# Second products summed in PSUM, and the transposes of x cut into pieces, in a fused attention and feed-forward kernel

## The chip, the cores and the metric

The kernel runs on one core of one Trainium2 chip. The metric is the device time of one execution in microseconds. Three runs of the kernel before took 543.70, 538.14 and 542.87 us, median 542.87. TensorE does the matrix products, VectorE (DVE), ScalarE (ACT) and GpSimd (POOL) do the elementwise work, and SyncE (SP), ACT and POOL issue the DMAs.

## The reference

There are 8 batches of 448 tokens, 12 heads of width 64, and a model width of 768.

```python
scores = q @ k.transpose(0, 1, 3, 2) / sqrt(64)
attn   = maximum(scores, 0) ** 2 / 448
x      = (attn @ v), heads side by side           # 8 x 448 x 768
xn     = (x - mean(x)) / sqrt(var(x) + 1e-6) * g_ln
out    = x + maximum(xn @ w_ch1, 0) @ w_ch2       # 768 -> 3072 -> 768
```

All inputs and the output are fp32; the kernel computes its products in bf16.

## The kernel before, in words

Batches go in four pairs of 896 tokens. The order of all instructions is written by hand: each engine and each DMA queue runs its own in the order in which the program emits them, and waits for the others by semaphores.

Attention leaves x transposed, `xT`, with the model width on the partitions. The first layer reads it so. The output needs x with tokens on the partitions, 7 tiles of 128 tokens by 6 chunks of 128, so `tokens(pair)` (L635) transposes all 42 blocks of a pair with one DMA on SP's queue into `xtok`, a pool with one buffer. `statistics` (L643) makes mean and variance of a tile on DVE from it, `roots` the scale `rstd`; the scale is applied to the output of the second layer.

Pair 0's first layer is computed directly. Pairs 1 to 3 use `ffn1_pair` (L757): for each of 12 steps `n`, seven block products in place of eight, with sums of blocks of x (`start`, made by DVE, L789) and of blocks of the weights. Pair 1 makes the weight sums and stores them in DRAM (`kept`); pairs 2 and 3 fetch them again, the "early" ones on ACT's queue from step 3 on, the "late" ones on SP's (`fetch`, L783). In `run` (L915) three products are gathered in an SBUF tile `z` (L922 to L926), and DVE writes `z` minus a product back into that product's PSUM bank (L938, L941), onto which the last two products accumulate. After each step `between` may add work: `between_two` and `between_three` put the statistics of pairs 2 and 3 there, one tile to a step.

The second layer of pairs 0 and 1 is direct (`ffn2_units`) and lies beside the attention of pairs 1 and 2. That of pairs 2 and 3 uses seven products too: `ffn2_mid` does the middle token tile 3, then `ffn2_pair` (L1042) does the tile pairs (0, 4), (1, 5) and (2, 6). A product is 12 matmuls (L1061) and has two units, halves of six. In `ffn2_pair` the products come in the order 3, 2, 5, 4, 1, 6, 7, with sums held in five output buffers, eight for pair 3 (`next_out`); ACT copies three of them out of PSUM (L1128, L1133, L1137), DVE adds (L1130, L1141, L1146), POOL subtracts and adds (L1142, L1143), and the four results are scaled and added to x on ACT and POOL (L1121, L1122) and on DVE (L1118, L1152, L1155), then stored by SP. The last tile pair has an order of its own, `finish_early`. Sums of the ReLU output that the next tile pair needs (`following`, h_sums_of) are made by DVE as their places come free.

Pair 2's seven-product second layer lies beside the attention of pair 3. `interleave` spreads two lists over each other: the units of the second layer, and the bundles of attention, three score steps each (L365 scores, L376 ReLU on ACT, L380 or L378 square, L397 values, L403 eviction into `xT`). The hooks "even" and "odd" are emitted after the third and the fifth of six groups of heads. The last `few` = 5 units are held back until attention is done and `start` of the next first layer has made the sums of x. Then `tokens(pair + 1)` is issued, and `run` begins. Pair 3's second layer runs by itself at the end.

Of the kernel before, what the change touches and what calls it, by code (L numbers as in the profile page):

```python
# [9 lines left out]
ALU = mybir.AluOpType  # L10
# [18 lines left out]
def kernel(  # L29
# [22 lines left out]
    nc = tc.nc  # L52
    P = 128
# [30 lines left out]
    xtpool = ctx.enter_context(tc.tile_pool(name="xt", bufs=1))  # L84
# [84 lines left out]
    hold = xtpool.tile([P, K1, NT, P], bf16, tag="xtok", name="hold_sb")  # L169
    hold = hold.rearrange("p c t d -> p (c t d)")  # L170
# [463 lines left out]

    def tokens(pair):  # L635
        xtok[pair] = xtpool.tile([P, K1, NT, P], bf16, tag="xtok", name="xtok_sb")
        rstd[pair] = spool.tile([P, NT], fp32, tag="rstd", name="rstd_sb")
        moments[pair] = spool.tile([P, NT, nc.vector.BN_AGGR_DIM], fp32, tag="mv", name="mv")
        nc.sync.dma_start_transpose(
            xtok[pair].rearrange("p c t d -> p (c t) d"),  # L640
            xT[pair].rearrange("p c s -> p (c s)"))
# [365 lines left out]
    def ffn2_mid(pair, a, b):  # L1007
# [22 lines left out]
        for names in (("s2", "s5"), ("s1",), ("s6",), ("s7",)):  # L1030
            h_sums_of(pair, 0, names)
# [10 lines left out]
    def ffn2_pair(pair, t, two_banks, last):  # L1042
# [5 lines left out]
        fp = next_out  # L1048

        def banks():  # L1050
            return (ps[:, :DH] for ps in two_banks())
# [15 lines left out]
        def scaled_on(o, left, right, row, half=None):  # L1067
            u = t + 4 * row
            if half is not None:
                right = xtok[pair][:, :, u, half * HP:(half + 1) * HP]  # L1070
                o, left = (z.rearrange("p (c d) -> p c d", d=D) for z in (o, left))
            nc.vector.scalar_tensor_tensor(
                o, left, rstd[pair][:, u:u + 1], right, op0=ALU.mult, op1=ALU.add)

        def out_of(z, row, half):
            store(pair, t + 4 * row, slice(half * DH, (half + 1) * DH), z, (nc.sync, nc.scalar))

        def finish_early():


            a, b = banks()
            yield from product(3, a)
            d, e, c12, c21, q_ = (fp() for _ in range(5))
            o12, o21 = next_out(), next_out()
            nc.scalar.copy(d, a)
            yield from product(2, b)
            nc.vector.tensor_sub(d, d, b)
            yield from product(5, a, False)
            nc.scalar.copy(c12, a)
            nc.gpsimd.tensor_sub(e, d, c12)  # L1090
            scaled_on(o12, a, None, 0, 1)
            out_of(o12, 0, 1)
            yield from product(4, b, False)
            nc.scalar.copy(c21, b)
            nc.gpsimd.tensor_add(e, e, c21)
            scaled_on(o21, b, None, 1, 0)
            out_of(o21, 1, 0)
            a, b = banks()
            yield from product(1, a)
            nc.vector.tensor_add(q_, a, d)  # L1100
            scaled_on(q_, q_, None, 1, 1)
            scaled_on(e, e, None, 0, 0)
            yield from product(6, b)
            scaled_on(q_, b, q_, 1)
            out_of(q_, 1, 1)
            yield from product(7, a, False)
            scaled_on(e, a, e, 0)
            out_of(e, 0, 0)

        if last:  # L1110
            yield from finish_early()
            return

        def result(eng, z, row, half):
            u = t + 4 * row
            z3, x = z.rearrange("p (c d) -> p c d", d=D), xtok[pair][:, :, u, half * HP:(half + 1) * HP]
            if eng is nc.vector:
                eng.scalar_tensor_tensor(  # L1118
                    z3, z3, rstd[pair][:, u:u + 1], x, op0=ALU.mult, op1=ALU.add)
            else:  # L1120
                nc.scalar.mul(z, z, rstd[pair][:, u:u + 1])  # L1121
                eng.tensor_add(z3, z3, x)  # L1122
            store(pair, u, slice(half * DH, (half + 1) * DH), z, (nc.sync, nc.sync))

        a, b = banks()
        yield from product(3, a)
        d = fp()
        nc.scalar.copy(d, a)  # L1128
        yield from product(2, b)
        nc.vector.tensor_sub(d, d, b)  # L1130
        yield from product(5, a, False)
        c12 = fp()
        nc.scalar.copy(c12, a)  # L1133
        yield from product(4, b, False)
        following("s2")
        c21 = fp()
        nc.scalar.copy(c21, b)  # L1137
        a, b = banks()
        yield from product(1, a)
        q_ = fp()  # L1140
        nc.vector.tensor_add(q_, a, d)  # L1141
        nc.gpsimd.tensor_sub(d, d, c12)  # L1142
        nc.gpsimd.tensor_add(d, d, c21)  # L1143
        following("s1")
        yield from product(6, b)
        nc.vector.tensor_add(q_, q_, b)  # L1146
        result(nc.gpsimd, q_, 1, 1)
        following("s6")
        result(nc.vector, c12, 0, 1)
        result(nc.vector, c21, 1, 0)  # L1150
# [33 lines left out]
    def token_units(pair):  # L1184
        return ([lambda: tokens(pair)] + [lambda t=t: statistics(pair, t) for t in range(NT)]
                + [lambda: roots(pair, 0, NT)])
# [177 lines left out]
```

## Time and profile before

| | us |
|---|---|
| median of three runs | 542.87 |
| the profiled execution | 543.38 |
| its span, first to last instruction | 540.2 |
| TensorE matmuls busy | 512.4 (95%) |
| VectorE busy | 386.1 (71%) |
| ScalarE busy | 316.7 (59%) |
| GpSimd busy | 129.7 (24%) |

The profile is of one execution. Busy times of an engine are summed over the span; matmuls are pipelined, so a busy TensorE can still be waiting inside. A row of a group gives its line, engine, operation and tiles, then busy time, mean duration and the idle time before it with what ended it. The list of waits names who waited for whom. The chain that ended last follows the execution back from its last instruction. A row of stages gives the busy time of each engine in a stretch of the span, the TensorE clock that was granted there as a share of the full one, and the busy share of the DMA engines.

### The profile page before, as it was taken

What the parts mean: (1) busy time and instruction counts of PE and PEld (TensorE: products, weight loads), DVE (VectorE), ACT (ScalarE), POOL (GpSimd) and SP (SyncE); (2) the same over time, 40 slices, a digit from 0 to 9 for tenths busy, and PEclk for the clock granted to TensorE, in tenths of its full rate; (3) what the DMA queues carried; (4) which work ended last, traced back from release to release, by engine and by line L of the source; (5) the groups of instructions that cost most, each with busy time, mean ns of one, the idle gap of its engine ahead of it and who ended that gap; (6) DMA issues with size and microseconds to landing.
All of it is one profiled execution on the core that took longest, in us unless ns stands there. A gap on an engine that the chain in (4) does not pass through costs nothing.

```text
span 540.2 us, 11478 instructions
## 1 busy us (share of the span) xinstructions
PE 512.4 (95%) x4565; PEld 301.3 (56%) x4565; DVE 386.1 (71%) x718; ACT 316.7 (59%) x512; POOL 129.7 (24%) x167
## 2 busy tenths in 40 slices
PE   8999999999999999999999969999989895999996
PEld 6677779655555555555555435545444442555663
DVE  5775754598998888678876858866866755865773
ACT  6966774688683676565462547669778062671110
POOL 7434101111221565011012690002320200000331
PEclk9999999999999999999999999999999897999999
DMA  9999999999899766159749984119872395411123
GB/s 197 206 205 208 210 179 165 167 166 193 157 178 177 155 203 159 52 94 181 147 92 177 200 179 112 52 30 159 130 128 60 98 167 130 133 51 27 33 58 89
DMA packets 124390, 74.34 MB, mean 138 GB/s; under 512 B 79794, under 2 KB 120754, under 8 KB 124338
## 3 DMA queue, kind: packets, MB, share of 16 engines
q1 hardware_dynamic: 93906, 42.16, 39.1%
q0 software_dynamic: 26976, 25.50, 32.0%
q10 hardware_dynamic: 3456, 5.97, 4.5%
q8 instruction: 35, 0.57, 0.4%
q14 instruction: 17, 0.14, 0.1%
HBM read 63.70 MB, written 16.91 MB: 149 GB/s over the span
## 4 chain that ended last, share of the span: by engine, by line
PE 81%; DMA 6%; ACT 6%; DVE 4%; issue 2%; SPq 0%; ACTq 0%; DVEq 0%
PE m_ps L847 23%; PE o_ps L728 20%; PE m_ps L1061 8%; PE h_ps L669 7%; PE sc_ps L365 6%; PE av_ps L397 5%; ACT attn_sb L376 4%; PE o_ps L1061 3%; DMA xtok_sb<-xT_sb 3%; PE o_ps L1017 3%; PE h_ps L713 2%; DMA room<-kept 2%; PE h_ps L695 1%; ACT early L376 1%; DMA w_sum<-kept 1%
## 5 line engine op out<-in xcount | busy, mean ns | idle before, releaser
L376 ACT ACTIVATE attn_sb<-sc_ps 128x896 bf16<-128x896 f32 (+4 forms) x150 | 126.0, 901 | 45.0 <-PE sc_ps L365 39.4
L728 PE MATMUL o_ps<-w,hT_sb 128*128 128x384 bf16 x672 | 116.0, 326 | 0.0
L851 ACT ACTIVATE hT_sb<-m_ps 128x448 bf16<-128x448 f32 x144 | 78.3, 544 | 62.3 <-PE m_ps L847 59.6
L728 PEld LDWEIGHTS <-hT_sb 128*128 128x128 bf16 x672 | 63.0, 98 | 48.8 <-issue 10.1
L380 DVE TENSOR_TENSOR attn_sb<-attn_sb 128x896 bf16<-128x896 bf16 x98 | 61.3, 637 | 30.6 <-ACT attn_sb L376 30.0
L669 PE MATMUL h_ps<-x_room,w 128*128 128x256 bf16 (+2 forms) x384 | 43.8, 263 | 0.4 <-ACT early L376 0.3
L1061 PEld LDWEIGHTS <-hT_sb 128*128 128x128 bf16 x288 | 28.0, 98 | 23.3 <-issue 5.6
L847 PE MATMUL m_ps<-x_sum,w 128*128 128x448 bf16 x144 | 33.9, 357 | 7.0 <-DVE x_room L924 7.0
L938 DVE TENSOR_TENSOR m_ps<-x_room,m_ps 128x448 f32<-128x448 f32 x36 | 22.6, 629 | 22.8 <-ACT hT_sb L851 22.5
L847 PEld LDWEIGHTS <-w_sum 128*128 128x128 bf16 x240 | 23.4, 98 | 26.6 <-DMA w_sum<-kept 5.1
L669 PEld LDWEIGHTS <-w 128*128 128x128 bf16 x384 | 33.8, 97 | 7.3 <-issue 2.9
L403 DVE TENSOR_SCALAR xT_sb<-av_ps 128x896 bf16<-128x896 f32 (+2 forms) x30 | 27.0, 900 | 14.5 <-PE av_ps L397 14.4
L847 PEld LDWEIGHTS <-w 128*128 128x128 bf16 x216 | 21.1, 98 | 27.4 <-issue 7.8
L646 DVE BATCH_NORM_STATS2 stats<-xtok_sb 128x6 f32<-128x384 bf16 x56 | 28.4, 549 | 9.9 <-DMA xtok_sb<-xT_sb 9.9
L159 POOL DMA_DIRECT2D k_sb<-in_k_dram x15 | 10.7, 712 | 100.5 <-DMA kT_sb<-k_sb 79.8
L159 POOL DMA_DIRECT2D v_sb<-in_v_dram x20 | 14.3, 715 | 82.5 <-PE sc_ps L365 72.2
L922 ACT COPY x_room<-m_ps 128x448 f32<-128x448 f32 x36 | 19.1, 532 | 24.6 <-PE m_ps L847 24.0
L1061 PEld LDWEIGHTS <-x_room 128*128 128x128 bf16 x216 | 20.5, 98 | 18.0 <-issue 5.2
L365 PE MATMUL sc_ps<-qT_sb,kT_sb 64*64 64x448 bf16 x392 | 28.8, 358 | 1.1 <-ACT attn_sb L376 0.9
L397 PE MATMUL av_ps<-attn_sb,v_sb 64*64 64x448 bf16 (+2 forms) x532 | 27.2, 331 | 1.1 <-DVE attn_sb L380 0.6
L679 ACT ACTIVATE hT_sb<-h_ps 128x256 bf16<-128x256 f32 (+1 forms) x49 | 18.1, 368 | 16.0 <-PE h_ps L669 15.1
L378 ACT ACTIVATE attn_sb<-attn_sb 128x896 bf16<-128x896 bf16 x28 | 26.6, 950 | 0.9
(213 smaller groups left out, 868.4 us busy)
## 6 DMA issues: line engine op xcount, KB each, us to landing
out_dram<-o_room SPq DMA_DIRECT2D x82, 96.0 KB, 2.3
w<-in_moe_w_ch_dram POOLq DMA_DIRECT2D x12, 384.0 KB, 13.9
w<-in_moe_w_ch_dram POOLq DMA_DIRECT2D x4, 1152.0 KB, 20.2
q_sb<-in_q_dram POOLq DMA_DIRECT2D x20, 224.0 KB, 5.6
v_sb<-in_v_dram POOLq DMA_DIRECT2D x20, 224.0 KB, 5.6
k_sb<-in_k_dram POOLq DMA_DIRECT2D x15, 224.0 KB, 5.2
w_room<-kept SPq DMA_DIRECT2D x12, 192.0 KB, 3.2
kept<-room SPq DMA_DIRECT2D x4, 480.0 KB, 2.8
```

Source lines behind the costliest of these rows:

```text
L365: nc.tensor.matmul(ps[cols, r, o * w:(o + 1) * w], g["k"](i)[rows, cols], g["q"](i, r)[rows, blk[0]:sum(blk), cols], start=True, stop=True)
L376: nc.scalar.activation(a, ps[:, :, :len(slots) * w], ACTF.Relu)
L378: nc.scalar.activation(a, a, ACTF.Square)
L380: nc.vector.tensor_mul(a, a, a)
L397: nc.tensor.matmul(ps[cols, hh, :w], v_sb[rows, pr, j * D:(j + 1) * D], g["attn"][i][rows, r, :], start=(j == 0), stop=(j == J - 1))
L403: nc.vector.tensor_scalar_mul(x, ps[:, :, :w], score_scale)
L646: nc.vector.bn_stats(stats[:, n], xtok[pair][:, n * G:(n + 1) * G, t, :])
L669: nc.tensor.matmul(ps[:, :w + more], w1[:, c, ni * P:(ni + 1) * P], xc[b][:, c, s.start:s.stop + more], start=(c == 0), stop=(c == K1 - 1))
L728: nc.tensor.matmul(ps[:, :DH], hT[pair][:, ki, t * P:(t + 1) * P], w2[:, ki, cols], start=(o == 0), stop=(o == K2 - 1))
L847: nc.tensor.matmul(ps, *at, start=(first and c == 0), stop=(c == KQ - 1), skip_group_check=not first)
L851: nc.scalar.activation(hT[pair][:, n + KH * row, half * S:(half + 1) * S], ps, ACTF.Relu)
L1061: nc.tensor.matmul(ps, x[:, ki], y[ki] if isinstance(y, list) else y[:, ki], start=(first and ki == 0), stop=(ki == KH - 1), skip_group_ch ...
```

## The change

`ffn2_pair` takes the products in the order 1, 4, 3, 2, 5, 6, 7, for all tile pairs alike. Products 1, 4 and 3 are added up in one fp32 tile `z` in SBUF; product 2 accumulates onto 4 in its bank and product 5 onto 3, which gives two of the four results. DVE then writes `z` minus each of these banks back into it, and products 6 and 7 accumulate onto that, which gives the other two. Each result is one DVE operation from PSUM into an output buffer. The two tiles for `z` take the place of two output buffers, the five further ones of pair 3 are gone, and three remain.

The room of the transposed x is one fixed tile now. Pair 1's transpose stays whole. Those of pairs 2 and 3 go in pieces: for pair 2, tiles 0 to 2 at the hook "even" (six DMAs), tiles 3 to 6 two chunks at a time just before `run` and after its steps 0 and 1; for pair 3, tiles 0 and 1 at "odd", tiles 3 to 5 after steps 0 and 1, tile 2 after step 2 and tile 6 after step 3. The statistics of pair 3 start after step 3 and take the tiles in the order 0, 1, 3, 4, 5, 2, 6.

The middle tile makes the sum s1 first. Beside pair 3's attention one bundle is emitted before the first unit, and four units instead of five are held back.

```diff
-    xtpool = ctx.enter_context(tc.tile_pool(name="xt", bufs=1))
...
-    hold = xtpool.tile([P, K1, NT, P], bf16, tag="xtok", name="hold_sb")
-    hold = hold.rearrange("p c t d -> p (c t d)")
+    xt_room = wpool.tile([P, K1, NT, P], bf16, tag="xtok", name="xtok_sb")
+    hold = xt_room.rearrange("p c t d -> p (c t d)")
...
+    def tokens_part(pair, lo, hi, chunks):
+
+        for c in chunks:
+            nc.sync.dma_start_transpose(xt_room[:, c, lo:hi], xT[pair][:, c, lo * P:hi * P])
+
     def tokens(pair):
-        xtok[pair] = xtpool.tile([P, K1, NT, P], bf16, tag="xtok", name="xtok_sb")
+        tokens_room(pair)
+        nc.sync.dma_start_transpose(
+            xt_room.rearrange("p c t d -> p (c t) d"), xT[pair].rearrange("p c s -> p (c s)"))
+
+    def tokens_room(pair):
+        xtok[pair] = xt_room
         rstd[pair] = spool.tile([P, NT], fp32, tag="rstd", name="rstd_sb")
         moments[pair] = spool.tile([P, NT, nc.vector.BN_AGGR_DIM], fp32, tag="mv", name="mv")
-        nc.sync.dma_start_transpose(
-            xtok[pair].rearrange("p c t d -> p (c t) d"),
-            xT[pair].rearrange("p c s -> p (c s)"))
...
-        for names in (("s2", "s5"), ("s1",), ("s6",), ("s7",)):
-            h_sums_of(pair, 0, names)
+        for name in ("s1", "s2", "s6", "s7"):
+            h_sums_of(pair, 0, (name,))
...
-    def ffn2_pair(pair, t, two_banks, last):
+    def ffn2_pair(pair, t, two_banks, z, last):
...
-        fp = next_out
-
-        def banks():
-            return (ps[:, :DH] for ps in two_banks())
+        a, b = (ps[:, :DH] for ps in two_banks)
...
-        def scaled_on(o, left, right, row, half=None):
-            u = t + 4 * row
-            if half is not None:
-                right = xtok[pair][:, :, u, half * HP:(half + 1) * HP]
-                o, left = (z.rearrange("p (c d) -> p c d", d=D) for z in (o, left))
...
+        def result(ps, row, half):
+            u, o = t + 4 * row, next_out()
+            o3, ps3 = (x.rearrange("p (c d) -> p c d", d=D) for x in (o, ps))
             nc.vector.scalar_tensor_tensor(
-                o, left, rstd[pair][:, u:u + 1], right, op0=ALU.mult, op1=ALU.add)
-
-        def out_of(z, row, half):
-            store(pair, t + 4 * row, slice(half * DH, (half + 1) * DH), z, (nc.sync, nc.scalar))
-
-        def finish_early():
...
-        if last:
-            yield from finish_early()
-            return
-
-        def result(eng, z, row, half):
...
-        a, b = banks()
+                o3, ps3, rstd[pair][:, u:u + 1], xtok[pair][:, :, u, half * HP:(half + 1) * HP],
+                op0=ALU.mult, op1=ALU.add)
+            store(pair, u, slice(half * DH, (half + 1) * DH), o, (nc.sync, nc.scalar if last else nc.sync))
+
+        yield from product(1, a)
+        nc.scalar.copy(z, a)
+        following("s1")
+        yield from product(4, b)
+        nc.vector.tensor_add(z, z, b)
         yield from product(3, a)
-        d = fp()
-        nc.scalar.copy(d, a)
-        yield from product(2, b)
-        nc.vector.tensor_sub(d, d, b)
+        nc.vector.tensor_add(z, z, a)
+        yield from product(2, b, False)
+        result(b, 1, 0)
+        nc.vector.tensor_sub(b, z, b)
         yield from product(5, a, False)
-        c12 = fp()
-        nc.scalar.copy(c12, a)
-        yield from product(4, b, False)
+        result(a, 0, 1)
+        nc.vector.tensor_sub(a, z, a)
         following("s2")
-        c21 = fp()
-        nc.scalar.copy(c21, b)
-        a, b = banks()
-        yield from product(1, a)
-        q_ = fp()
-        nc.vector.tensor_add(q_, a, d)
-        nc.gpsimd.tensor_sub(d, d, c12)
-        nc.gpsimd.tensor_add(d, d, c21)
-        following("s1")
-        yield from product(6, b)
-        nc.vector.tensor_add(q_, q_, b)
-        result(nc.gpsimd, q_, 1, 1)
+        yield from product(6, b, False)
+        result(b, 1, 1)
         following("s6")
-        result(nc.vector, c12, 0, 1)
-        result(nc.vector, c21, 1, 0)
-        d3, x = d.rearrange("p (c d) -> p c d", d=D), xtok[pair][:, :, t, :HP]
-        nc.vector.scalar_tensor_tensor(
-            d3, d3, rstd[pair][:, t:t + 1], x, op0=ALU.mult, op1=ALU.add)
         yield from product(7, a, False)
-        nc.vector.scalar_tensor_tensor(
-            d, a, rstd[pair][:, t:t + 1], d, op0=ALU.mult, op1=ALU.add)
-        store(pair, t, slice(0, DH), d, (nc.sync, nc.sync))
+        result(a, 0, 0)
         following("s7")
...
-    def token_units(pair):
-        return ([lambda: tokens(pair)] + [lambda t=t: statistics(pair, t) for t in range(NT)]
-                + [lambda: roots(pair, 0, NT)])
+    def token_units(pair, order):
+        return [lambda t=t: statistics(pair, t) for t in order] + [lambda: roots(pair, 0, NT)]
...
-                        tokens=token_units(2)[1:])
+                        tokens=token_units(2, range(NT)))
...
+        if n < 2:
+            tokens_part(2, 3, NT, range(2 * n + 2, 2 * n + 4))
+        elif n > 2 and side["tokens"]:
+            side["tokens"].pop(0)()
+
+    def between_three(n):
+        if n == 0:
+            side.update(tokens=token_units(3, (0, 1, 3, 4, 5, 2, 6)))
+        if n < 4:
+            tokens_part(3, *((3, 6, range(3)), (3, 6, range(3, K1)), (2, 3, range(K1)), (6, 7, range(K1)))[n])
         if n > 2 and side["tokens"]:
             side["tokens"].pop(0)()
 
-    def between_three(n):
-        if n == 0:
-            side.update(tokens=token_units(3)[1:])
-        if n > 1 and side["tokens"]:
-            side["tokens"].pop(0)()
+    soon = {(1, "even"): (0, 3, range(K1)), (1, "run"): (3, NT, range(2)), (2, "odd"): (0, 2, range(K1))}
...
-                yield from ffn2_pair(pair, t, lambda: banks(t), pair == pairs - 1 and t == 2)
+                yield from ffn2_pair(pair, t, banks(t), zs[t % 2], pair == pairs - 1 and t == 2)
...
-            following[name]()
+                if pair:
+                    tokens_room(pair + 1)
+            if name != "run":
+                following[name]()
+            if (pair, name) in soon:
+                tokens_part(pair + 1, *soon[pair, name])
         if last:
             mm = [ps_mm.tile([P, 512], fp32, tag="mm", name="o_ps") for _ in range(2)]
-            outs += [x_room.rearrange("p b c s -> p (b c s)")[:, 3 * KH * P:3 * KH * P + 2 * DH].bitcast(fp32),
-                     room0[:, 9:].rearrange("p c n -> p (c n)").bitcast(fp32)]
+            zs = [x_room.rearrange("p b c s -> p (b c s)")[:, 3 * KH * P:3 * KH * P + 2 * DH].bitcast(fp32),
+                  room0[:, 9:].rearrange("p c n -> p (c n)").bitcast(fp32)]
...
-        few = 5 if last else 3
-        interleave(units[:-few], beside)
+        few = 4 if last else 3
+        interleave(units[:-few], beside, 0, 1 if last else 0)
...
         stage = following
-        tokens(pair + 1)
+        if pair == 0:
+            tokens(pair + 1)
+        hook("run")
         stage["run"]()
...
-    z = late[0].tile([P, 5, DH], fp32, tag="z", name="z_sb")
-    outs[3:] = [z[:, i] for i in range(5)]
```

39 lines of the change are left out of this document (1 added, 38 removed).

## The prediction

> **What bounds the kernel now.** I read the busy shares first, then cut the span by stages. The windows below are, in order: the seven-product first layer of pair 1, of pair 2 and of pair 3; the attention of pair 3 beside the second products of pair 2; two stretches right after a PE stall; the second products of pair 3 alone; and the attention of pair 2 beside the second layer of pair 1. Columns: window, length, busy us and count of PE, weight loads, DVE, ACT and POOL, granted clock, DMA share, GB/s.
>
> ```profile
> core 0: us, PE busy (x) PEld busy (x) DVE busy (x) ACT busy (x) POOL busy (x), PEclk, DMA share, GB/s
> 175.17:221.95 46.78, 46.78 (x249) 24.13 (x247) 38.69 (x74) 30.86 (x57) 23.63 (x32) 1.00 0.63 164
> 297.02:349.53 52.51, 47.36 (x248) 23.88 (x247) 39.72 (x76) 30.95 (x58) 23.29 (x25) 1.00 0.68 140
> 429.54:485.93 56.39, 49.41 (x248) 24.88 (x247) 37.55 (x71) 30.93 (x58) 0.54 (x1) 0.92 0.56 118
> 356.94:429.54 72.60, 65.24 (x598) 33.91 (x598) 52.04 (x71) 53.37 (x68) 14.61 (x16) 0.99 0.60 110
> 426.74:431.20 4.46, 4.46 (x17) 2.20 (x17) 3.79 (x5) 0.91 (x2) 3.18 (x3) 0.62 0.00 1
> 451.70:455.10 3.40, 3.40 (x10) 1.36 (x10) 2.76 (x5) 1.08 (x2) 0.00 (x0) 0.50 0.28 73
> 494.70:535.90 41.20, 41.12 (x254) 24.56 (x251) 25.45 (x34) 5.54 (x11) 10.32 (x8) 1.00 0.26 59
> 222.00:297.02 75.02, 75.02 (x679) 40.76 (x678) 56.49 (x104) 38.81 (x52) 9.30 (x13) 1.00 0.71 126
> ```
>
> TensorE sets the time: in most stages it is busy to the last tenth. The three first layers do the same matmuls, yet take 46.78, 52.51 and 56.39 us. So pair 2 loses 5.73 us and pair 3 9.61 us against pair 1; the first is all idle time, the second partly a low clock. The list of what PE waited for, and the chain of work that ended last (start, us, what), say on what.
>
> ```profile
> PE m_ps L847 <- DVE x_room L924: 7.0, 1, 7.0
> PE m_ps L847 <- DMA w_sum<-kept: 4.2, 2, 2.3
> PE o_ps L1061 <- DVE o_room L1141: 2.7, 1, 2.7
> PE o_ps L1061 <- ACT o_room L1133: 2.0, 2, 1.4
> ...
> PE sc_ps L365 <- ACT attn_sb L376: 0.9, 4, 0.3
> PE m_ps L847 <- DMA room<-kept: 0.9, 1, 0.9
> ...
> PE o_ps L1061 <- DVE room L739: 0.6, 1, 0.6
> ```
>
> ```profile
> 300.12 8.80 DMA room<-kept
> 308.96 3.88 PE m_ps L847 x20
> 312.85 6.14 DMA w_sum<-kept
> ...
> 414.17 0.69 PE sc_ps L365 x12
> 414.86 3.05 PE o_ps L1061 x18
> 418.47 1.14 PE o_ps L1061 x6
> 419.61 1.48 PE av_ps L397 x28
> 421.11 1.10 DVE xT_sb L403
> 422.52 0.55 issue
> 423.06 3.16 DVE x_sum L789 x4
> 426.74 3.01 PE o_ps L1061 x12
> ...
> 435.15 14.72 DMA xtok_sb<-xT_sb
> 449.89 1.03 DVE stats L646 x2
> 451.07 0.59 DVE x_room L924
> ```
>
> Three places, then. In pair 2 the weight sums come back from DRAM too late, 8.80 and 6.14 us each. In pair 3 DVE stands at the statistics of tile 0, whose transpose took 14.72 us, and L924, which PE needs, is queued behind them. At 422 to 427 DVE makes the five sums of x first, and L1141, which must leave a PSUM bank before the last product goes into it, comes after. The two transposes are the same instruction:
>
> ```profile
> L639 SPq DMA_TRANSPOSE xtok_sb<-xT_sb x4: 6557/9304/12465, 83.9 to 435.1; - x4
> DMA to landing us min/median/max: 8.3/14.3/18.2
> L312 SPq DMA_TRANSPOSE kT_sb<-k_sb x10: 1223/1270/1412, 72.5 to 397.5; - x10
> ```
>
> One transpose of x is 42 blocks of 128x128 and holds SP for 6.6 to 12.5 us, 0.16 to 0.30 us a block, and lands in 8.3 to 18.2 us. Pair 1's stage carries it without loss, since it stores weight sums there and fetches none.
>
> **Term 1, pair 2's first layer.** The change issues 18 of the 42 blocks at the middle of the attention before, 8 where the whole transpose stood, and 8 each after steps 0 and 1. SP waits for nothing between the first two eights, so 16 blocks go at once: 16 x 0.30 = 4.8 us of SP instead of 12.5, and at the slowest landing (18.2 / 42 = 0.43 us a block) 6.9 us of full DMA engines instead of 18.2. The fetch that took 8.80 us missed its product by 0.9 us; with under half of the blocks beside it, it should be in time. The next ones, which missed by 4.2 us in two waits, had SP or the DMA engines still full of transposes at 312 us; the last eight blocks now end near 310. I take 0.7 us as left: **-5.0 us**. The bounds are -5.7 (nothing left) and -2.5 (24 of the 42 blocks, 24 / 42 of the loss, still there). The six early pieces lie beside pair 1's second layer, where PE is busy 75.02 of 75.02 us. They put 18 x 0.30 = 5.4 us on SP ahead of stores and of transposes of keys; the three output buffers turn over once in three results, some 16 us (14 results in 75 us), so this stays hidden. Without that cover it would cost at most those 5.4 us.
>
> **Term 2, pair 3's first layer.** Tiles 0 and 1 come at the last hook of the attention, tiles 3 to 5 after steps 0 and 1, tiles 2 and 6 after steps 2 and 3, and the statistics start a step later in an order that leaves 2 and 6 for the end. None should meet a missing transpose. That returns the 7.0 us wait and the clock after it: 3.40 us at 0.50 is 1.7 us lost. The stage also begins with the clock of the stall before it (4.46 us at 0.62 is 1.7 us, about half of it, 0.8, behind 429.54). 7.0 + 1.7 + 0.8 = 9.5 of the 9.61.
>
> The page "TensorE: Matmul & The Clock Gate" of the Trainium skill (Part 1: The HAM clock gate) says that the clock halves only after an idle window of about 3.4 us. The trace shows 0.62 after a wait of 2.7 us. By the page that wait need have cost no clock, and the sum would come out 1.7 us smaller; I go by the row.
>
> What is late next: after the last values product DVE has 1.10 (L403), five sums at 3.16 / 4 = 0.79, two results at 0.61 and L924 at 0.62, 6.9 us in all; PE has 24 matmuls at 41.20 / 252 = 0.163 and 12 at 46.78 / 252 = 0.186, 6.1 us, before the product that needs L924. So 0.8 us come back as a wait, and 0.3 for the fetches of the weight sums that queue on SP behind nine blocks. **-8.5 us**, between -9.6 and -4.5 (rival A).
>
> **Term 3, the attention of pair 3.** Its matmuls need 252 x 0.163 = 41.2, 14 triples of scores at 0.69 = 9.7, six values products at 1.48 = 8.9 and the middle's last nine, 1.5: 61.3 us of the 72.60. Of the 11.3 us over, 2.7 + 2.0 + 0.9 + 0.6 are waits listed above and 0.9 is the clock after 426.74; some 4 us are changes of shape and small gaps that stay.
>
> ```profile
> L1130 DVE TENSOR_TENSOR o_room<-o_room,o_ps 128x384 f32<-128x384 f32 x2 | 1.1, 552 | 0.8 <-ACT o_room L1128 0.8
> L1155 DVE SCALAR_TENSOR_TENSOR o_room<-o_ps,rstd_sb,o_room 128x384 f32<-128x384 f32 x2 | 1.2, 612 | 0.1
> L1133 ACT COPY o_room<-o_ps 128x384 f32<-128x384 f32 x3 | 1.4, 467 | 1.7 <-DMA out_dram<-o_room 1.7
> L1121 ACT ACTIVATE x_room<-x_room,rstd_sb 128x384 f32<-128x384 f32 x1 | 0.6, 616 | 0.1
> ```
>
> For each tile pair ACT had three copies at 0.47 and a scaling at 0.62, now one copy: 1.56 us less, 4.7 in the stage. POOL's three operations go. DVE had seven, three at 0.55 and four at 0.61, 4.1 us; now it has two sums and two seeds at 0.55 and four results at 0.61, 4.65 us. The seeds write PSUM, as L938 and L941 do in every first layer, and products 6 and 7 wait for them.
>
> Gone are the 2.0 us behind L1133 (the copy and its full output buffer no longer exist) and the 2.7 + 0.9 at the end: four units instead of five remain there, products 6 and 7, whose seeds are issued before the sums of x. Half of the 0.9 us that scores wait for ACT goes with ACT's lighter load, 0.5. Against that: result and seed take 1.2 us of DVE beside a product of 12 x 0.163 = 1.96, so a seed is late when DVE is over 0.8 us behind. I put 0.7 us for it (bounds 0, and rival D); the early bundle of scores may wait for the last ReLUs of the stage before, 0 to 0.6 us, in that too. **-5.4 us**, between -7.9 and 0.
>
> The second products of pair 3 alone have PE busy 41.12 of 41.20 us and end, before and after, in one DVE operation and a store: 0. Pair 2's product order needs the sum s1 first instead of none; it is made during the middle product.
>
> Sum: 5.0 + 8.5 + 5.4 = 18.9 us. The profiled execution took 543.38 us, so 524.5; the median of the runs is 0.5 us lower: **524 us**.
>
> **The rivals.** A: small transposes cost as much as larger ones. The rows show 0.16 to 0.30 us a block, and 1.27 us for seven blocks is the shortest whole transpose. If a one-block piece also took 1.27, the 18 pieces of pair 3's steps 0 to 3 would hold SP for 22.9 us where those steps last 15.6; the weight sums of steps 5 and 6 would come about 2 us late each, and clock is lost: +5, **529 us**. The page "DMA: Bandwidth & Descriptors" of the Trainium skill (Rules for kernel authors) speaks for it: it wants small transfers joined, since under 64 KB most is overhead, and a block is 32 KB. No transpose under seven blocks is in this trace. Against it: 42 blocks take no less per block than seven.
>
> B: the attention stage keeps its length; waits for scores and squares take the place of those removed. ACT is busy there 53.37 of 72.60 us, which leaves room, but the chain runs through it often. Term 3 is 0: **529.5 us**.
>
> C: the change does not do what it says, because x's one room is guarded as a whole: results that read other tiles wait until the pieces land. 18 and 12 blocks at 0.43 with 2 us of landing are 9.7 and 7.2 us of waiting DVE, and most of terms 1 and 2 is given back: **540 us**. Against it, one tile's parts are kept apart now:
>
> ```profile
> 301.99 0.62 DVE L926 TENSOR_TENSOR x_room<-x_room,m_ps 128x448 f32<-128x448 f32 x1
> 302.13 0.35 PE L847 MATMUL m_ps<-x_room,room 128*128 128x448 bf16 x1
> ```
>
> DVE writes one part of x_room while PE reads another.
>
> D, the slower side: the seeds. Four products of each tile pair now wait for DVE, twelve waits in pair 3's attention, and DVE is queued behind squares that wait for ACT. Should each cost what the longest PE wait for such an operation cost, 2.7 us, that is 12 x 2.7 = 32 against 19.6 us of gains: **556 us**. It decides from 1.6 us a wait. Against it: L1130 had the same slack of one product and is in no PE wait.
>
> **How the numbers follow.** Forecast 0.60, A 0.12, B 0.14, C 0.07, D 0.07. The three runs before lie 5.6 us apart, so about 1%, 5.4 us, is what a measurement can tell from no change. Forecast, A and B are faster by more, 0.86; C is within it, 0.07; D slower, 0.07. All lower bounds together give 5.7 + 9.6 + 7.9 = 23.2, 520; with a little of the spread of the runs the range is 519 to 532, which holds the forecast, A and B.
>
> **What would show it.** The first layers of pairs 2 and 3 should last 47 to 48.5 us each, with no wait for kept weight sums or for x's transposes; the granted clock should stay at 1.00 from 420 us on; the attention of pair 3 should last 67 us, with no ACT copy but one per tile pair. I am wrong if PE waits for the seeds (D), if SP's pieces take over 0.6 us each (A), or if results wait for a transpose (C).

## The result, and the profile after

The changed kernel takes 535.58 us (median of 20 runs, 533.66 to 540.33) and the kernel before 542.15 us in the runs beside it. The ratio is 0.9894, with a 95% interval of 0.987 to 0.9918. The forecast was 524 us with a range of 519 to 532, so the sign was right and a third of the gain came: 6.6 us of 18.9.

The profiled execution took 538.45 us with a span of 536.5, 3.7 us less than the span before. It is 2.9 us above its own median, so it shows the losses a little larger than they are on the middle. All stages below run from one first matmul to the next. In the kernel before these starts lie at 297.02 (first layer of pair 2), 349.37 (middle tile, which opens the attention of pair 3), 429.54 (first layer of pair 3) and 485.77 us (second products of pair 3). The rows of the kernel after are those four stages in order, with three stretches right after a stall in between; columns as in the prediction.

```profile
297.11:348.85 51.74, 48.62 (x247) 24.43 (x246) 40.50 (x76) 30.77 (x58) 23.23 (x25) 0.97 0.59 139
348.85:424.99 76.14, 71.81 (x643) 38.23 (x642) 53.66 (x78) 51.76 (x63) 5.03 (x7) 0.98 0.55 96
424.99:482.21 57.22, 50.48 (x248) 24.90 (x246) 37.49 (x72) 30.50 (x58) 0.00 (x0) 0.94 0.50 129
432.10:436.50 4.40, 4.39 (x15) 1.91 (x16) 1.24 (x2) 0.90 (x2) 0.00 (x0) 0.61 0.93 278
455.50:458.70 3.20, 3.20 (x12) 1.39 (x12) 2.99 (x6) 2.36 (x5) 0.00 (x0) 0.69 0.48 123
363.40:367.60 4.20, 4.19 (x25) 1.72 (x25) 1.73 (x3) 2.53 (x3) 0.00 (x0) 0.64 0.52 117
482.21:536.50 54.29, 50.05 (x307) 29.84 (x305) 30.00 (x42) 3.25 (x7) 0.00 (x0) 0.99 0.21 51
```

| us | before | after | change | predicted |
|---|---|---|---|---|
| first layer of pair 2 | 52.35 | 51.74 | -0.6 | -5.0 |
| attention of pair 3 | 80.17 | 76.14 | -4.0 | -5.4 |
| first layer of pair 3 | 56.23 | 57.22 | +1.0 | -8.5 |
| second products of pair 3 | 54.4 | 54.29 | -0.1 | 0 |

The two first layers, which were to give 13.5 us, gave nothing. The -0.6 is of one profile: the kernels further down whose order is the same up to there have pair 2's first layer at 49.1 to 52.6 us, which is -3.2 to +0.2. The list of what PE waited for in the kernel after shows that most of the old waits did go, and what stands in their place.

```profile
PE m_ps L853 <- DMA w_room<-kept: 3.5, 1, 3.5
PE o_ps L1064 <- DVE o_room L745: 3.2, 1, 3.2
PE m_ps L853 <- ACT x_room L928: 2.8, 1, 2.8
PE m_ps L853 <- DMA w_sum<-kept: 2.0, 1, 2.0
PE m_ps L853 <- DVE x_room L930: 1.6, 2, 1.1
...
PE sc_ps L364 <- ACT hT_sb L857: 0.6, 1, 0.6
```

The 7.0 us for L924 (now L930) are 1.6 in two waits, and the waits for L1133 and L1141 are gone with those lines. Of the 4.2 + 0.9 us for pair 2's weight sums 2.0 are left. No wait for a seed (L1087, L1090) is in the list. New are a fetch of weight sums that is late by 3.5 us, the eviction of the middle tile (L745), late by 3.2, and ACT's copy L928, late by 2.8. All three are followed by a low clock: 0.61, 0.64 and 0.69 in the windows above. These three figures are one thing seen through windows of different place and length: behind each wait the trace has one stretch of 3.41 us at 0.50, which costs 1.7 us, with full clock around it.

**Where the late fetch comes from.** These are all pieces of the kernel after (count, then least, median and longest time on SP in ns; below it the time to landing), and SP's queue around the start of pair 3's first layer (start, us, what).

```profile
L637 SPq DMA_TRANSPOSE xtok_sb<-xT_sb x36: 1099/1244/2113, 268.6 to 458.4; - x36
...
DMA to landing us min/median/max: 2.2/3.0/7.7
```

```profile
419.58 7.70 SPq L637 DMA_TRANSPOSE xtok_sb<-xT_sb  x6
427.39 1.17 SPq L756 DMA_DIRECT2D out_dram<-o_room  x2
428.79 2.31 SPq L789 DMA_DIRECT2D w_room<-kept  x5
...
444.00 7.53 SPq L637 DMA_TRANSPOSE xtok_sb<-xT_sb  x6
451.63 0.52 SPq L789 DMA_DIRECT2D w_room<-kept  x1
452.20 7.47 SPq L637 DMA_TRANSPOSE xtok_sb<-xT_sb  x6
```

The six pieces at the hook "odd" have two blocks each and hold SP for 7.70 us, 1.28 each; the six at 444.00 have one block each and hold it for 7.53, 1.26 each. A piece has a price of its own of about 1.25 us, and whether it holds one block or two hardly shows in it. The pieces at "odd" stand right ahead of the five fetches of `start`, which so are issued at 428.79, after the first layer has begun at 424.99. PE and ACT then read (two timelines):

```profile
432.11 1.75 PE L853 MATMUL m_ps<-xT_sb,w_room 128*128 128x448 bf16 x6 [3.50 <-DMA w_room<-kept]
...
455.48 1.38 PE L853 MATMUL m_ps<-x_sum,w 128*128 128x448 bf16 x6 [2.78 <-ACT x_room L928]
```

```profile
454.47 0.33 ACTq L789 DMA_DIRECT2D w_room<-kept  x1
454.89 0.53 ACT L928 COPY x_room<-m_ps 128x448 f32<-128x448 f32 x1 [4.45 <-DMA xtok_sb<-xT_sb]
```

ACT issues its share of the fetches in order with its copies. The fetch at 454.47 waited for the landing of a piece, the first of the six that SP issues from 452.20 on: 452.20 plus the shortest landing of 2.2 us is 454.4. It needs nothing of that piece. In the trace's list of instructions the DMAs of SP and ACT share eight semaphores, and the fetch waits on number 118, which it is to raise itself and which that piece, landed at 454.45, raised before it. The copy behind the fetch was 4.45 us late, and PE behind the copy 2.78.

**Where the late eviction comes from.** DVE and PE at the start of the attention:

```profile
355.79 0.62 DVE L379 TENSOR_TENSOR attn_sb<-attn_sb 128x896 bf16<-128x896 bf16 x1 [4.74 <-ACT attn_sb L375]
...
358.15 1.75 DVE L1005 TENSOR_TENSOR x_room<-hT_sb 128x3072 bf16<-128x3072 bf16 x1
...
362.75 1.13 DVE L745 SCALAR_TENSOR_TENSOR o_room<-o_ps,rstd_sb,xtok_sb 128x384 f32<-128x384 f32 x2
```

```profile
354.36 0.76 PE L364 MATMUL sc_ps<-qT_sb,kT_sb 64*64 64x448 bf16 x12 [0.63 <-ACT hT_sb L857]
...
363.41 1.14 PE L1064 MATMUL o_ps<-w,x_room 128*128 128x384 bf16 x6 [3.15 <-DVE o_room L745]
```

The bundle of scores that is emitted before the first unit puts squares (L379) on DVE, which wait for ACT. The sums of the ReLU output (L1005 to L1011) come behind them, and L745, which frees the bank for the first product, behind those.

### The profile page after: what moved, and what is told of

It is laid out like the page before. It is cut to its first block, busy times and chain, and to the rows that moved or that the text cites. A ratio compares the mean times of both kernels' runs of the same rounds, so it can differ in the third digit from the quotient of the medians.

```text
span 536.5 us, 11444 instructions
## 1 busy us (share of the span) xinstructions
PE 514.6 (96%) x4565; PEld 302.4 (56%) x4565; DVE 384.0 (72%) x723; ACT 308.9 (58%) x495; POOL 109.7 (20%) x150
## 4 chain that ended last, share of the span: by engine, by line
PE 88%; DVE 3%; ACT 3%; DMA 2%; SPq 2%; issue 2%; ACTq 0%
PE m_ps L853 26%; PE o_ps L734 19%; PE m_ps L1064 8%; PE h_ps L675 7%; PE o_ps L1064 7%; PE sc_ps L364 7%; PE av_ps L396 6%; PE o_ps L1023 2%; PE h_ps L719 2%; PE h_ps L701 2%; ACT early L375 1%; DMA w_sum<-kept 1%; ACT attn_sb L375 1%; PE tr_ps L249 1%; PE idle_ps L235 1%
## 5 line engine op out<-in xcount | busy, mean ns | idle before, releaser
L379 DVE TENSOR_TENSOR attn_sb<-attn_sb 128x896 bf16<-128x896 bf16 x98 | 59.8, 621 | 32.8 <-ACT attn_sb L375 32.2
L928 ACT COPY x_room<-m_ps 128x448 f32<-128x448 f32 x36 | 19.1, 532 | 37.0 <-PE m_ps L853 31.4
L930 DVE TENSOR_TENSOR x_room<-x_room,m_ps 128x448 f32<-128x448 f32 x36 | 21.6, 600 | 10.0 <-ACT x_room L928 5.9
```

The source lines that it names most:

```text
L379: nc.vector.tensor_mul(a, a, a)
```

## Experiments

Theory after the result: three places, each by itself, keep the gain away. They are the early bundle (attention), the pieces at "odd" ahead of the fetches (start of pair 3's first layer), and the number of pieces on SP (later in that layer, and in pair 2's). Rivals: the new products or the transposes in pieces give little by themselves; or there is one loss only, which any repair moves on.

**Without the early bundle.**

```diff
-        interleave(units[:-few], beside, 0, 1 if last else 0)
+        interleave(units[:-few], beside)
```

> The changed kernel without the one bundle of scores ahead of the first unit; all else as changed. Theory: the early bundle puts two squares, which wait for ACT, ahead of the sums of the ReLU output and so ahead of the eviction of the middle tile on DVE; the 3.2 us PE wait for L745, the 0.6 us wait for the ReLU and the clock after them (4.2 us at 0.64, 1.5 us) go: the attention of pair 3 from 71.3 to about 67 us, the time 4.5 us under the changed kernel. Rival: the wait comes of s1 being made apart and first, which makes the sums no shorter; then a wait of over 2 us stays and the time moves under 1.5 us.

Measured: 531.43 us, ratio to before 0.9808 (0.9759 to 0.9856). The attention row, and two of PE's waits, without the bundle:

```profile
346.33:418.80 72.47, 69.73 (x644) 37.60 (x642) 53.75 (x78) 51.52 (x63) 5.04 (x7) 1.00 0.58 101
```

```profile
PE m_ps L853 <- DMA w_room<-kept: 3.8, 1, 3.8
...
PE o_ps L1064 <- DVE o_room L745: 1.9, 1, 1.9
```

The attention falls from 76.14 to 72.47 us and keeps its clock. So the bundle costs 3.7 us in these two profiles, about 1.7 of them lost clock, and the change to the attention without it is worth 80.17 - 72.47 = 7.7 us. The wait for L745 was expected to go, but only fell from 3.2 to 1.9: two squares and the four sums still stand ahead of it. The late fetch is still there.

**The new products alone, transposes whole as before** (no early bundle; four held-back units). The main lines of the diff; the pieces after the steps go too.

```diff
...
-    soon = {(1, "even"): (0, 3, range(K1)), (1, "run"): (3, NT, range(2)), (2, "odd"): (0, 2, range(K1))}
+    soon = {}
...
-        if pair == 0:
-            tokens(pair + 1)
-        hook("run")
+        tokens(pair + 1)
```

> The new products and seeds alone, with four units held back, no early bundle, and the transposes of x whole, as before. Theory: the products are worth some 9 us in the attention of pair 3 (72.6 to about 64 to 66 us from the first scores to the first layer of pair 3) and nothing elsewhere, the first layers of pairs 2 and 3 stay at 52.5 and 55.5 to 56.5 us: about 8 to 9 us under the kernel before. Rival: what the changed kernel gained it gained by the pieces, and the seeds wait for DVE: within 2 us of the kernel before.

Measured: 532.08 us, ratio 0.9793 (0.9743 to 0.9842). The attention is 72.48 us, as above, and the first layers 53.43 and 52.79. The time is 12.1 us under the kernel before, where 8 to 9 were expected: the new products take 3.4 us from pair 3's first layer too (56.23 to 52.79), which was to stay. The old waits for the weight sums and behind the statistics are back, the second shorter than the 7.0 us of before:

```profile
PE m_ps L853 <- DMA w_sum<-kept: 4.6, 2, 3.2
PE m_ps L853 <- DVE x_room L930: 4.2, 2, 3.8
```

**The pieces alone, on the products of before** (with the later statistics and their order; the old output buffers). The last lines of a longer diff, against the kernel before; the rest is that of the change's pieces.

```diff
...
-        tokens(pair + 1)
+        if pair == 0:
+            tokens(pair + 1)
+        hook("run")
```

> The kernel before with its own products, and only the transposes of x in pieces with the later statistics. Theory: each piece holds SP for about 1.25 us whatever its size, the lumps of six hold back the fetches of weight sums, and the gain of no whole transpose is spent on that: first layers of pairs 2 and 3 near 52 and 56 to 58 us, time within 2 us of the kernel before. Rival: the pieces are worth the 13.5 us that the prediction had for them, and the new products lose it: first layers near 47 to 48.5 us, time 12 us under.

Measured: 536.8 us, ratio 0.989 (0.9849 to 0.993). First layers 49.22 and 53.98 us, attention 78.88. Neither side of the expectation came: 7.4 us under the kernel before is more than the 2 us of the theory and less than the 12 of the rival. The first of PE's waits is now

```profile
PE m_ps L853 <- ACT x_room L928: 4.2, 1, 4.2
```

and no late fetch of `start` is in the list: with the old products SP issues the pieces of "odd" at 408.12 and the fetches at 417.76, before the layer begins at 425.30. In the changed kernel eight stores, from 403.76 on, hold SP until the pieces at 419.58. Products alone gain 2.1%, pieces alone 1.1%, and together, in the changed kernel, they gain 1.1%. With both but without the bundle (the first experiment) it is 1.9%. So the bundle takes 0.8%; what else products and pieces do to each other the next experiment takes up.

**The pieces of tiles 0 and 1 of pair 3 earlier**: issued behind the last result of tile pair 1, in place of the hook "odd".

```diff
+        if (pair, t) == (2, 1):
+            tokens_part(3, 0, 2, range(K1))
...
-    soon = {(1, "even"): (0, 3, range(K1)), (1, "run"): (3, NT, range(2)), (2, "odd"): (0, 2, range(K1))}
+    soon = {(1, "even"): (0, 3, range(K1)), (1, "run"): (3, NT, range(2))}
```

> The changed kernel with the six pieces of tiles 0 and 1 of pair 3 issued right after the last result of the second tile pair, some 7 us earlier in SP's order, instead of at the hook. Theory: the six pieces held SP from 419.6 to 427.3 us, so the first fetches for pair 3 were issued at 428.8; now they are issued at about 421.5, the 3.5 us PE wait for them and the clock after it (4.4 us at 0.61, 1.7 us) go, pair 3's first layer from 57.4 to about 52.5 us, the time 5 us under the changed kernel. Rival: the fetch was late because the DMA engines were full, or its room came free late; then the wait stays above 2 us.

Measured: 531.65 us, ratio 0.9791 (0.9752 to 0.9829). SP's queue:

```profile
406.07 8.60 SPq L637 DMA_TRANSPOSE xtok_sb<-xT_sb  x6
416.87 3.06 SPq L756 DMA_DIRECT2D out_dram<-o_room  x4
420.17 2.31 SPq L789 DMA_DIRECT2D w_room<-kept  x5
```

The five fetches go out 8.6 us earlier than in the changed kernel, the wait of 3.5 us is gone, and pair 3's first layer falls from 57.22 to 50.63. What is left there is ACT's copy behind the landing of a piece, 3.2 us. The attention, with the bundle still in it and the same wait for L745, is 74.51 us, since the clock held this time. So 2.0 of the bundle's 3.7 us are waiting, and the rest is clock that was lost in one profile and not in the other.

**Both repairs**: the two diffs above together.

> Both repairs at once: no early bundle of scores, and the pieces of tiles 0 and 1 of pair 3 issued before start's fetches are due. Alone they gave 531.4 and 531.7 us where the changed kernel takes 535.6, so 4.2 and 3.9. Theory (two causes at two places, the middle tile at 363 us and the seam before pair 3's first layer at 432 us): they add, 535.6 - 4.2 - 3.9 = 527.5 us, attention stage of pair 3 near 72 us, first layer of pair 3 near 50.6 us. Rival (one loss, which either repair moves the end past): no more than 4.2 together, 531.4 us, and one of the two stages falls back.

Measured: 528.2 us, ratio 0.9709 (0.9672 to 0.9746); attention 72.47, first layer of pair 3 52.35 us. They add within 0.7 us: 535.6 - 4.2 - 3.9 = 527.5 was expected. The layer is 1.7 us longer than with the pieces moved alone, since the wait for ACT was 3.5 us and lost clock this time (six matmuls in 2.40 us, 1.30 at full clock):

```profile
444.88 2.40 PE L853 MATMUL m_ps<-x_sum,w 128*128 128x448 bf16 x6 [3.48 <-ACT x_room L928]
```

**Fewer pieces for pair 3**: tiles 2 to 6 in six pieces of five blocks after steps 0 and 1, in place of 18 pieces of one to three blocks after steps 0 to 3. The six early ones of tiles 0 and 1 stay. This is on top of both repairs. (The text on record counts those six among the pieces replaced; the difference of twelve is right.)

```diff
-            side.update(tokens=token_units(3, (0, 1, 3, 4, 5, 2, 6)))
-        if n < 4:
-            tokens_part(3, *((3, 6, range(3)), (3, 6, range(3, K1)), (2, 3, range(K1)), (6, 7, range(K1)))[n])
+            side.update(tokens=token_units(3, range(NT)))
+        if n < 2:
+            tokens_part(3, 2, NT, range(3 * n, 3 * n + 3))
```

> As the kernel with both repairs, but tiles 2 to 6 of pair 3 come in six pieces of five blocks after steps 0 and 1, in place of 24 pieces of one to three blocks after steps 0 to 3. Theory (a piece costs about 1.25 us of SP whatever its size, and ACT's fetch waits for the landing of a piece issued some DMAs before it): 12 pieces fewer are 15 us less of SP, the 3.2 us that PE waits behind ACT's fetch at some 455 us goes, first layer of pair 3 47.5 to 48 us in place of 50.6, time 524.5 to 525 us. Rival (what counts is the blocks, not the pieces): the 30 blocks come earlier and denser, ACT's fetch still waits 4 us or more, first layer 50 us or more, 527 us or more.

Measured: 524.18 us, ratio 0.9631 (0.959 to 0.9672). All pieces of this kernel, and the first layer of pair 3:

```profile
L637 SPq DMA_TRANSPOSE xtok_sb<-xT_sb x24: 1190/1264/2196, 268.6 to 434.6; - x24
```

```profile
422.17:469.34 47.17, 46.70 (x249) 24.07 (x247) 37.31 (x72) 30.73 (x58) 0.00 (x0) 1.00 0.59 136
```

The median piece still takes 1.26 us, twelve are gone, ACT waits for none, and the layer takes 47.17 us, as long as pair 1's 46.78. So the number of blocks does not make the loss. Whether it is the number of pieces, or that none is issued after steps 2 and 3 any more, these runs do not part; the edit changed both, and the order of the statistics.

**Pair 2 in six pieces of seven blocks**, none at "even", on the kernel with fewer pieces.

```diff
-            tokens_part(2, 3, NT, range(2 * n + 2, 2 * n + 4))
+            tokens_part(2, 0, NT, range(2 * n + 2, 2 * n + 4))
...
-    soon = {(1, "even"): (0, 3, range(K1)), (1, "run"): (3, NT, range(2))}
+    soon = {(1, "run"): (0, NT, range(2))}
```

> As the kernel with fewer pieces, but pair 2's transpose goes in six pieces of seven blocks, two before the first layer, two each after steps 0 and 1, and none at the hook in the attention before. Theory (the six early pieces push SP and make the fetch of the weight sums at 294 us 1.3 to 2 us late): that fetch is issued near 293.7 us again, PE's wait of 0.9 to 2.8 us at 302 us goes, first layer of pair 2 47.5 to 48.5 us in place of 49.2 to 51.8, time 522 to 524 us. Rival (the early pieces are harmless, and 14 blocks at once ahead of the first steps hold up the fetches of the weight sums as the whole transpose did): first layer of pair 2 51 to 53.4 us, time 525 us or more.

Measured: 524.13 us, ratio 0.9635 (0.9593 to 0.9677), no gain; first layer of pair 2 51.71 us. First SP in the changed kernel, with the early pieces, then in this one; then what ACT waited for here, and the stretch behind PE's wait:

```profile
268.56 8.20 SPq L637 DMA_TRANSPOSE xtok_sb<-xT_sb  x6
...
288.22 3.54 SPq L316 DMA_TRANSPOSE qT_sb<-q_sb  x1
...
295.76 2.59 SPq L789 DMA_DIRECT2D w_sum<-kept  x4
```

```profile
293.74 2.17 SPq L789 DMA_DIRECT2D w_sum<-kept  x4
...
299.69 8.86 SPq L637 DMA_TRANSPOSE xtok_sb<-xT_sb  x4
```

```profile
ACT x_room L928 <- DMA xtok_sb<-xT_sb: 4.2, 1, 4.2
```

```profile
310.00:313.00 3.00, 3.00 (x9) 1.16 (x8) 2.30 (x5) 1.76 (x4) 3.00 (x5) 0.52 1.03 234
```

Half of the theory held: without the early pieces the fetch goes out 2.0 us earlier and PE's wait for it is gone. But four pieces now hold SP for 8.86 us, ACT's fetch waits 4.2 us for the landing of one, PE waits 2.6, and the clock is 0.52 behind it. One wait has taken the place of the other. Again the fetch (308.42) shares its semaphore with the piece (issued at 299.69, landed at 308.39).

**The sums of the middle tile moved**, on the kernel with fewer pieces.

```diff
-        for name in ("s1", "s2", "s6", "s7"):
-            h_sums_of(pair, 0, (name,))
+        h_sums_of(pair, 0, ("s1",))
...
             finish(pair, 3, half, 0, K1, ps, (nc.sync, nc.sync))
+        for name in ("s2", "s6", "s7"):
+            h_sums_of(pair, 0, (name,))
```

> As the kernel with fewer pieces, but the middle tile makes the sum s1 alone before its last products, and s2, s6 and s7 of the first tile pair after its two results. Theory (the eviction of the middle tile stands behind four sums on DVE, and PE waits 1.9 us for its bank): that wait goes, attention stage of pair 3 70.5 to 71 us in place of 72.5, time 1.5 to 2 us under the kernel with fewer pieces. Rival (the sums only move the wait): product 2 waits for s2 or the scores wait for a square, the stage stays at 72 us or more, no gain.

Measured: 522.07 us, ratio 0.9599 (0.9559 to 0.9638). The attention is 71.71 us, 0.8 less and not 1.5 to 2: two squares that wait for ACT still stand ahead of L745, and PE waits 1.1 us for it in place of 1.9. The median is 2.1 us lower than with fewer pieces alone, but the intervals overlap, so 0.8 is what is shown.

**Pair 2's pieces later**, on the kernel with the sums moved: six of seven blocks, two after each of steps 0 to 2, and in a second kernel three after each of steps 1 and 2 (shown). The statistics start after step 4.

```diff
-        if n < 2:
-            tokens_part(2, 3, NT, range(2 * n + 2, 2 * n + 4))
-        elif n > 2 and side["tokens"]:
+        if 1 <= n < 3:
+            tokens_part(2, 0, NT, range(3 * (n - 1), 3 * (n - 1) + 3))
+        elif n > 3 and side["tokens"]:
...
-    soon = {(1, "even"): (0, 3, range(K1)), (1, "run"): (3, NT, range(2))}
+    soon = {}
```

> As the kernel with the sums of the middle tile moved, but pair 2's transpose goes in six pieces of seven blocks, two after each of steps 0, 1 and 2 of its first layer, none before it, and the statistics start after step 4. In the kernel with six pieces from before the first layer on, the DMA engines were over 1.1 busy of 16 from 296 to 314 us, and a fetch by ACT waited 4.2 us there. Theory (it is the pile of transposes on full DMA engines that makes fetches of pair 2 late, first those of SP, then those of ACT): spread over three steps none is late, PE waits under 1 us between 300 and 320 us, first layer of pair 2 47 to 48.5 us, time 518.5 to 520 us against 522.1. Rival (ACT's fetch waits for a transpose eight DMAs before it wherever that stands): PE still waits 2 us or more behind it and loses clock, first layer 50 us or more, 521 to 523 us.

> The same, but three pieces of seven blocks after each of steps 1 and 2, so that the first starts when the DMA engines are done with the stores of the stage before. Theory of the pile: no worse than two after each of steps 0, 1 and 2, or 1 us better, 518 to 520 us, first layer of pair 2 47 to 48.5 us. Rival: as there, 521 to 523 us; and a third case, the last piece lands after 320 us, DVE stands at the statistics of tile 0 as in the kernel before, and PE waits for DVE: first layer 49 us or more.

Measured: 520.78 us, ratio 0.9607 (0.9579 to 0.9635), and 519.59 us, ratio 0.9595 (0.9565 to 0.9626). The first has its layer at 48.11 us, with PE waits of 0.4 and 0.6 us for fetched sums. Both layers are as the theory of the pile had them, and ACT waits for no piece in either kernel. The stages of the second, in the order of the table, and the longest of PE's waits:

```profile
297.36:344.48 47.12, 47.00 (x249) 24.01 (x246) 40.99 (x75) 30.70 (x57) 23.22 (x25) 1.00 0.62 157
344.48:416.20 71.72, 69.73 (x643) 37.60 (x642) 53.81 (x79) 51.71 (x64) 5.03 (x7) 1.00 0.63 115
416.20:463.37 47.17, 46.70 (x249) 24.07 (x247) 37.30 (x72) 30.78 (x58) 0.00 (x0) 1.00 0.62 136
```

```profile
PE o_ps L1065 <- DVE o_room L745: 1.1, 1, 1.1
```

The third case of that expectation is there only as a trace, DVE waits 0.8 us for a piece at the statistics and PE for none of it. Both first layers are now at the length of pair 1's, the clock is 1.00 in all three stages, and this kernel beats both the kernel before and the changed one: 52.35 - 47.12 = 5.23, 80.17 - 71.72 = 8.45 and 56.23 - 47.17 = 9.06, together 22.7 us. Against the kernel with the sums moved, both ratios are within the noise; there the gain is shown by the stage alone (49.13 us in one profile of it).

## Why the prediction was wrong

**What bounded the kernel** was read rightly. Three stages had the losses that were named, and taking nearly all of them away is worth 22.7 us in the profile of the last kernel. The sum of the best bounds was 23.2.

**Term 1 (-5.0, measured -0.6) failed in holding the early pieces hidden.** "16 x 0.30 = 4.8 us of SP" and "18 x 0.30 = 5.4 us" took the long transpose's time per block, where a piece costs about 1.25 us. For the 16 blocks that did not matter, four pieces took 5.32 us. The six at "even" took 8.20 us in place of 5.4, and "so this stays hidden" did not come true: in the seven kernels with these pieces the fetch of the weight sums (295.76 in the changed one) goes out 1.3 to 2.3 us before the layer's first matmul, and without them 3.0 to 3.4. The wait that was to shrink to 0.7 was 2.0, with a stretch of lost clock behind it; it is 0.9 to 2.8 in the seven. Undoing the early pieces alone did not help, since the pieces right ahead of the first steps then held up ACT. The gain of 5.2 us came when the pieces were few and came after the first fetches.

**Term 2 (-8.5, measured +1.0) failed twice, at SP's queue and at ACT's.** The mechanism, statistics that meet no missing transpose, came as said: the 7.0 us went, and the 0.8 that was to come back at the start was 0.47 (the wait for L930 there). But the step "0.3 for the fetches of the weight sums that queue on SP behind nine blocks" looked at the pieces after the stage's start and not at the six at "odd", which stand ahead of the fetches of `start` on the same queue. They have 12 blocks, 3.6 us at 0.30, and took 7.70; PE waited 3.5 us and lost clock behind it. Moving them gave 6.6 us in the stage. And no step looked at ACT's queue, where a fetch can wait for a piece and hold the copies behind it: fewer and earlier pieces took away the rest. The stage then gave 9.1 us, between the 8.5 and the bound of 9.6.

**Term 3 (-5.4, measured -4.0) had two sizes off, on opposite sides.** The waits named did go, and the new products are worth 7.7 us without the bundle, near the bound of 7.9 (the 8.5 of the last kernel hold the moved sums too): "0.7 us" for late seeds was not needed. The bound's working is not given; the waits and the clock listed there are 7.1 us, so some of the 4 us that were to stay went as well. The early bundle was priced at 0 to 0.6 us by PE's wait for the last ReLUs. That wait was there, 0.63, but the bundle also put squares on DVE ahead of the middle tile's eviction, which the prediction did not follow: 3.7 us, or 2.0 where the clock held. That the term came near is luck, of two errors with opposite signs.

**Of the rivals,** A, given 0.12, was right in its price (1.27 us taken, 1.24 to 1.26 found) and in that it falls on fetches. It was put at 529 because only the 18 pieces of steps 0 to 3 were counted in it, and the late weight sums that it had for steps 5 and 6 did not come: PE waits for none there, but for ACT's copy. The Trainium skill's page "DMA: Bandwidth & Descriptors" (Rules for kernel authors), which wants small transfers joined, spoke for it; the rows of L637 agree, 1.24 us for pieces of 32 to 128 KB. B fell, as the attention did get shorter. C fell: no result (L745, L1073) waits for a piece in any kernel's list. D fell: in no kernel's list does PE wait for a seed (L1087 and L1090 in the changed one).

**The clock** was to be 1.00 from 420 us on. In the profile after it was lower behind the waits at 432 and 455 us, of 3.5 and 2.8 us, which the forecast did not have.

**The sum.** Products alone and pieces alone gain 2.1% and 1.1%; added up that is 3.2% or some 17 us, close to the 18.9 forecast. That the sums are close is luck: the pieces, forecast at 13.5, gave 7.4 us alone, and the products, forecast at 5.4, gave 12.1. Together they lost what came of where their DMAs and squares were put beside each other; with both repairs the ratio is 0.9709, a gain of 2.9%. The range had no case in which both SP's price and the bundle took from the gain at once.

## What to carry to other kernels

Price a DMA instruction by the instruction before pricing it by its bytes: look for the shortest row of its kind in the trace, and where none is short enough take that shortest row as the price. When a transfer is cut up, list for each queue what is then issued behind the pieces, compute engines that issue fetches among them, which DMAs share a semaphore with the pieces, and how long the pieces hold it. When work is emitted earlier, follow each engine it runs on to the next instruction that frees a bank or a buffer.

## What the runs showed of the hardware

A DMA transpose from SBUF to SBUF holds SP's queue for nearly the same time with one to five blocks of 128x128 in it: over all traces with pieces the medians are 1.23, 1.24, 1.25, 1.26 and 1.28 us for 1, 2, 3, 4 and 5 blocks. With seven it is 1.43, from 1.22 to 3.98 us, the longest where the transposes of pair 2 follow each other in the first steps of its layer. The one of 42 blocks held it for 6.6 to 12.6.

A wait's length alone does not settle whether the clock falls. In the changed kernel it is 0.64 after 3.15 us of waiting for L745; with the pieces of pair 3 moved, the same wait of 3.16 us leaves it at 1.00. And 1.97 us at 302 us in the changed kernel are followed by 0.51. But length does set the odds. The traces of all kernels here have 39 waits of PE of over 1 us after the first 60 us of the span: none of the 20 up to 1.88 us lost clock, nine of the 13 from 1.89 to 3.22 did, and all six from 3.48 us on. Each loss but one is a single stretch of 3.41 us at 0.50, which begins during the wait or within 1.4 us behind it; the wait of 6.98 us has 6.83. The rows are the stretches behind these waits, of the kernel with moved pieces and of the changed one:

```profile
363.50:367.70 4.20, 4.20 (x34) 2.22 (x34) 2.04 (x4) 2.69 (x4) 0.00 (x0) 1.00 0.53 118
```

```profile
303.20:306.60 3.40, 3.40 (x10) 1.37 (x9) 1.24 (x2) 1.08 (x2) 3.40 (x5) 0.51 1.27 213
```

The Trainium skill's page "TensorE: Matmul & The Clock Gate" (Part 1: The HAM clock gate) speaks of a window of about 3.4 us that runs on by itself and is not started by the kernel, which fits that equal waits end differently; that an idle window of that length is needed does not fit the 1.97 us. In the seven profiles of kernels with the same order up to pair 2's first layer, its wait for weight sums is 0.9 to 1.7 us in four, which keep their clock and take 49.1 to 49.2 us for the layer, and 2.0 to 2.8 us in three, which lose a stretch and take 51.7 to 52.6. Why the wait itself differs stays open. Open too is why the transpose of q at 288 us holds SP for 2.5 to 3.6 us in these seven (3.54 in the changed kernel), behind the early pieces, and 1.3 in the kernels without them.
